# Last sequence's spatial product from seven block products, in a kernel of chunked linear attention and a gated layer

## The chip, the cores and the metric

One core of a Trainium2 chip runs the whole program. The metric is device time in microseconds (us), from the launch of the program to its end; the profiler adds one execution with a trace. TensorE is called PE here, VectorE DVE, ScalarE ACT, GpSimd POOL, and SyncE, whose queue issues nearly all DMAs, SP. Each engine works through its own instructions in the order in which the program emits them, and waits on semaphores for the others.

## The reference, cut to what matters

Four sequences of 768 tokens go through a gated linear recurrence with 8 heads of 48 (complex gates, real output), and its output x, 384 features per token, through a gated layer:

```python
h = gelu(x @ w_in)                     # 384 -> 1024
u, v = h[..., :512], h[..., 512:]
v_n = (v - mean(v)) / sqrt(var(v) + 1e-06) * g_ln
v_s = einsum('ts,bsd->btd', w_sg, v_n) + b_sg[None, :, None]
out = x + (u * v_s) @ w_out            # 512 -> 384
```

w_sg is 768 x 768 and mixes the tokens of a sequence: v_s is the *spatial product* that the change is about. For one sequence it is a 768 x 768 by 768 x 512 product.

## The kernel before

The recurrence is worked in 24 chunks of 128 tokens, six to a sequence. Behind each sequence's attention comes its gated layer, with features on partitions and tokens along the row, in two halves of 384 tokens. Operands of large products are split in two: "high" holds the value rounded to the type that PE reads, "low" what is left. A product is then three passes (high·high, high·low, low·high), by the helper `mm3` (L228). All four sequences compute the spatial product alike: for each half and each of four feature tiles f, `spatial` (L820) runs 6 chunks x 3 passes = 18 matmuls of 128x128 by 128x384 into the PSUM tile `pvs`, 144 for a sequence. Then DVE makes tg = pvs·g + b (L848), multiplies by u (L851), `high` makes gh (L212) and `low` makes gl (L220), and PE multiplies both with w_out into `po`; DVE adds x (L868), and a DMA stores it (L871). `normal` (L763) loads a half of x, makes v, its gelu and layer norm, and vh/vl for each chunk; `expand` makes u. The layer norm's small steps (`rsqrt`, L721) run on POOL.

Nothing schedules this. Every piece of work is a generator, and the table ORDER (L33) says whose next step is emitted: a token names a generator, a count behind a colon takes several steps, one mark (') sends the step's flexible work to POOL and two marks to DVE; without one `high` goes to ACT and `low` to DVE. Names: a attend (attention of a chunk; DVE masks its scores in L657 as tile `am`), z heads (loads K and Q), v vbuf, n normal, x expand, y spatial and the output product, h gate_range and k weight_range. These last two check inputs: each loads 192 or 384 KB (`gr`, `wr`) through SP into one of two buffers with the tags "re" and "im", and reduces them to a column on DVE (L382, L385, L311) or ACT. At the end `ok` (L883 to L894, L1005) joins the columns; all engines read the flag `oki` and go on to a general version when it is not set. The attention output of a chunk is copied (`yp`), stored to DRAM (`xd`) and loaded back as x.

Of the kernel before, what the change touches and what calls it, by code (L numbers as in the profile page):

```python
# [9 lines left out]
F32 = mybir.dt.float32  # L10
F32R = mybir.dt.float32r
# [3 lines left out]
ALU = mybir.AluOpType  # L15
# [3 lines left out]
P = 128  # L19
# [54 lines left out]
a20 e11 s12 h15 h4 a20 h1 a20 a21 e11'' r22' r22:3 a20 y2_3 z23 a20'' a20 a21' a21:2 y2_3'' a21 h15 h22 a21 y2_3''  # L74
a21:2 x2_0:2 h5 m12 y2_3'' h22 h0 x2_0 y2_3 e12' y2_3 v23 z22 y2_0 h5' v22 y2_3 h2 a20' y2_0 x2_0 y2_3:3 y2_0'' e12
r22:3 x2_0 r22 y2_3 x2_0 y2_3 a20 y2_0 y2_0'' a21 z22 y2_0:2 z23 k7 y2_0:2' y2_0:3 a21 h0' a22:5 a22' a22 e12 h2'
a22:2 x2_0 a23 y2_0 a22 y2_3 h18 e12'' a22' a22 y2_0'' n3_0 a23:2 a23'' a22 n3_0' y2_0 a22 a23 n3_0' y2_0:2 a23:2
y2_0' n3_0 h18 n3_0:2 k10 h1' k10 n3_0:3 y2_0'' y2_0 n3_3 n3_0 n3_3 k7 n3_0 y2_0:2 n3_0 n3_3' h7 h7'' k12 y2_0:3 n3_0
k1 n3_0' y2_0 n3_0' y2_0 n3_0 y2_0 n3_3 n3_0' n3_0:2 n3_3 n3_0' n3_3 n3_0 n3_3 k12 n3_0 h6 n3_3:3 x3_3 n3_3 x3_3 n3_3
y2_0 x3_3:3 h19 x3_3 k1 x3_3 n3_3:2 n3_3' x3_0 h19 n3_3 n3_3:2' n3_3'' x3_3 h13 n3_3' n3_3'' n3_3 h23 k6 h13 x3_0:2 h6  # L80
h23 y3_3:2 y3_3:3'' y3_3:2 y3_3' y3_3:5 k6 k9 y3_3'' h14 y3_3' h14 y3_3 k4 k0 x3_0 y3_0 y3_3 y3_0 k3 x3_0 k4 y3_3'
x3_0 y3_3'' k9 y3_3' h12 y3_3:3 y3_0' k3 h12 y3_3:2 x3_0 y3_3:2 h21:2 y3_3 h16 h17 x3_0 y3_0'' h17 y3_0' y3_0:2 x3_0
y3_0'' y3_3 y3_0' k0 k11 y3_0 h3 h16 y3_0 ok x3_0 h3 y3_0 y3_0'' k11 ok y3_0 x3_0 y3_0 ok:2 y3_0:2 ok y3_0:3 ok y3_0:3
ok y3_0:9
"""


# [1 line left out]
def tile_kernel(ctx: ExitStack, tc: tile.TileContext, t_q, t_k, t_re, t_im, u_q, u_k, u_re, u_im, t_v, v, q, k, f_re, f_im,  # L89
                w_in, g_ln, w_sg, b_sg, w_out, out):  # L90
    nc = tc.nc


    B, S, H, D = v.shape
    DM = H * D
    NCH = S // P
    DFF = w_in.shape[-1]
    F = DFF // 2
    NK = DM // P
    NF = F // P  # L100
# [16 lines left out]
    gp = ctx.enter_context(tc.tile_pool(name="gp", bufs=1))  # L117
# [82 lines left out]
    def ew():  # L200

        return nc.gpsimd if alt[0] == 1 else nc.vector
# [7 lines left out]
    def high(h, src):  # L210

        if alt[0] == 0:  # L212
            act(h, src, AF.Copy)
        elif alt[0] == 1:
            nc.gpsimd.tensor_scalar(out=h, in0=src, scalar1=1.0, scalar2=1.0, op0=ALU.mult, op1=ALU.mult)
        else:
            nc.vector.tensor_copy(h, src)  # L217

    def low(l, src, h):
        ew().tensor_tensor(out=l, in0=src, in1=h.bitcast(F32), op=ALU.subtract)  # L220
# [539 lines left out]
        yield  # L760
        return x, xh, xl

    def normal(b, c0, m):  # L763

        x, xh, xl = yield from get_x(b, c0, m)
        mv = mp.tile([P, 2, MT // P], F32, tag="mv", name="mv")
        neg = mp.tile([P, MT // P], F32, tag="neg", name="neg")
        vrs = []
        for i in range(m):
            pv = psm.tile([P, F], F32, tag="m", name="pv")  # L770
            if b == 0:
                stoke(pv[:, 0:2 * P], 20 if c0 + i == NCH - m else 3)
            ts = slice(i * P, (i + 1) * P)
            mm3(pv, lambda kt: xh[:, kt, ts], lambda kt: xl[:, kt, ts],
                lambda kt: winh[:, kt, F:], lambda kt: winl[:, kt, F:], NK)
            yield
            vr = mp.tile([P, F], F32, tag="vr", name="vr", bufs=3)
            act(vr, pv, AF.Gelu_apprx_tanh)
            vrs.append(vr)
            yield  # L780
            stt = mp.tile([P, 6], F32, tag="bst", name="bst")
            nc.vector.bn_stats(stt, vr)  # L782
            nc.vector.bn_aggr(mv[:, :, i], stt)
            yield
        rs, sh = rsqrt(neg, mv, m)
        yield
        for i in range(m):
            s_ = c0 + i
            vr = vrs[i]
# [5 lines left out]
            yield  # L795
            vh = mp.tile([P, F], F32R, tag=f"vh{s_}", name=f"vh{s_}", bufs=1)
# [282 lines left out]
```

## Time and profile before

| | us |
|---|---|
| three timed runs | 423.67, 424.76, 426.26 |
| their median | 424.76 |
| profiled execution | 426.0 |
| its span on the core | 424.3 |
| PE busy | 408.2 (96%) |
| DVE busy | 342.3 (81%) |
| ACT busy | 278.6 (66%) |
| POOL busy | 152.0 (36%) |

Busy time counts matmuls as long as any is in the array, so that PE's gaps are what is left of the span. 1.7 us of the profiled execution lie outside its span. A row of the trace below names line, engine, operation, and output<-input tiles.

### The profile page before, as it was taken

Reading aid. Unit: us, or ns where it says so; the run is one execution under the profiler, and the core shown is the slowest. Engines: PE = TensorE matmul, PEld = TensorE weight load, DVE = VectorE, ACT = ScalarE, POOL = GpSimd, SP = SyncE. Lnnn points to the kernel's source line nnn. Section 1 sums busy time; section 2 is a strip of 40 time slices with the busy share of each in tenths; the row PEclk is TensorE's granted clock in tenths of the full one; section 3 lists DMA queues with packets and bytes.
Section 4 is the critical chain, followed back from the end, with each engine's and each line's share of the span. In section 5 each row is a group of like instructions: output and inputs, shape, how many; then the busy total and the mean of one; then the engine's idle time right before and its main releaser. Section 6 shows DMA issues by size and latency. Waiting matters only on the chain.

```text
span 424.3 us, 9760 instructions
## 1 busy us (share of the span) xinstructions
PE 408.2 (96%) x3806; PEld 370.9 (87%) x3806; DVE 342.3 (81%) x593; ACT 278.6 (66%) x392; POOL 152.0 (36%) x207
## 2 busy tenths in 40 slices
PE   7999998989999999999999999999999999999995
PEld 5567787878899998889989998989999988899994
DVE  4999989999998999896999698786974556575483
ACT  7899998999989677786896935876640212540010
POOL 2126348255241430625164722542121144233210
PEclk9999999999999999999999999999999999999999
DMA  6878869598397896988749888879669856563441
GB/s 198 266 224 250 231 183 289 161 283 260 108 289 247 235 320 161 289 279 255 215 145 280 248 260 241 267 221 288 147 192 276 246 173 192 153 225 112 157 133 61
DMA packets 77563, 92.93 MB, mean 219 GB/s; under 512 B 10564, under 2 KB 59462, under 8 KB 77512
## 3 DMA queue, kind: packets, MB, share of 16 engines
q1 hardware_dynamic: 77368, 92.16, 73.1%
q8 instruction: 31, 0.51, 0.5%
q14 instruction: 20, 0.16, 0.1%
q10 hardware_dynamic: 144, 0.10, 0.1%
HBM read 68.64 MB, written 23.60 MB: 217 GB/s over the span
## 4 chain that ended last, share of the span: by engine, by line
PE 57%; DVE 15%; DMA 10%; ACT 10%; POOL 3%; issue 3%; SPq 1%; DVEq 0%; POOLq 0%
PE pvs L231 18%; PE po L835 10%; PE pu L231 6%; PE pv L231 6%; PE pa L647 4%; PE py L704 3%; ACT L194 3%; PE py L709 3%; PE ps L673 2%; DMA K<-rk 2%; DMA vbuf<-in_t_v_dram 2%; ACT csn L195 2%; DVE bst L782 2%; ACT l L195 1%; DMA Q<-rq 1%
## 5 line engine op out<-in xcount | busy, mean ns | idle before, releaser
L231 PE MATMUL pvs<-wsgh,vh 128*128 128x384 f32 x192 | 65.3, 340 | 0.0
L231 PE MATMUL pvs<-wsgh,vl 128*128 128x384 f32 x192 | 64.8, 337 | 0.1
L231 PE MATMUL pvs<-wsgl,vh 128*128 128x384 f32 x192 | 64.5, 336 | 0.0
L194 ACT ACT_TABLE_LOAD x48 | 61.6, 1283 | 1.7 <-PEq L1064 0.9
L647 PE MATMUL pa<-Q,K 96*64 96x128 f32 (+1 forms) x768 | 41.5, 250 | 1.1 <-DVE am L657 0.9
L647 PEld LDWEIGHTS pa<-Q,K 96*64 96x64 f32 x768 | 36.9, 137 | 3.9 <-ACT csn L195 1.0
L704 PE MATMUL py<-am,vbuf 128*64 128x128 f32 x384 | 38.2, 275 | 0.6 <-DVE am L657 0.6
L231 PEld LDWEIGHTS pvs<-wsgh,vh 128*128 128x128 f32 x192 | 36.0, 188 | 1.0 <-issue 0.9
L231 PEld LDWEIGHTS pvs<-wsgh,vl 128*128 128x128 f32 x192 | 36.0, 188 | 0.6 <-DVE vl L220 0.6
L231 PEld LDWEIGHTS pvs<-wsgl,vh 128*128 128x128 f32 x192 | 36.1, 188 | 0.0
L657 DVE TENSOR_TENSOR am<-pa,masks 128x512 f32<-128x512 f32 x45 | 30.1, 680 | 5.2 <-PE pa L647 4.4
L709 PE MATMUL py<-Q,S 96*48 96x128 f32 x320 | 33.2, 272 | 0.1
L835 PE MATMUL po<-gh,wouth 128*128 128x384 f32 x96 | 32.9, 343 | 0.0
L835 PE MATMUL po<-gl,wouth 128*128 128x384 f32 x96 | 32.4, 337 | 0.4 <-DVE gl L220 0.4
L231 PE MATMUL pu<-xh,winh 128*128 128x384 f32 x96 | 32.7, 341 | 0.0
L835 PE MATMUL po<-gh,woutl 128*128 128x384 f32 x96 | 32.3, 336 | 0.0
L231 PE MATMUL pu<-xh,winl 128*128 128x384 f32 x96 | 32.3, 336 | 0.0
L231 PE MATMUL pu<-xl,winh 128*128 128x384 f32 x96 | 32.2, 336 | 0.0
L220 POOL TENSOR_TENSOR gl<-tg,gh 128x384 fp32r<-128x384 f32 x13 | 16.5, 1266 | 42.7 <-DVE gh L217 20.3
L231 PE MATMUL pv<-winh,xl 128*128 128x512 f32 x72 | 28.7, 398 | 1.8 <-POOL xl L220 1.1
L231 PE MATMUL pv<-winh,xh 128*128 128x512 f32 x72 | 29.3, 406 | 1.1 <-DVE xh L217 0.7
L231 PE MATMUL pv<-winl,xh 128*128 128x512 f32 x72 | 28.5, 396 | 0.0
(253 smaller groups left out, 1066.6 us busy)
## 6 DMA issues: line engine op xcount, KB each, us to landing
vbuf<-in_t_v_dram SPq DMA_DIRECT2D x24, 288.0 KB, 5.5
K<-rk SPq DMA_DIRECT2D x18, 384.0 KB, 6.0
Q<-rq SPq DMA_DIRECT2D x18, 384.0 KB, 7.9
x<-xd SPq DMA_DIRECT2D x9, 576.0 KB, 5.1
xd<-yp SPq DMA_DIRECT2D x48, 96.0 KB, 3.3
gr<-in_f_im_dram SPq DMA_DIRECT2D x12, 384.0 KB, 4.0
out_dram<-x SPq DMA_DIRECT2D x23, 192.0 KB, 2.6
re<-in_u_re_dram SPq DMA_DIRECT2D x9, 384.0 KB, 5.9
```

The source lines that it names most:

```text
L194: nc.scalar.preload_act_table_set(SETS[t])
L195: nc.scalar.activation(out, in_, func, scale=scale, **kw)
L220: ew().tensor_tensor(out=l, in0=src, in1=h.bitcast(F32), op=ALU.subtract)
L231: nc.tensor.matmul(o, w(i), x(i), start=(i == 0 and j == 0), stop=(i == n - 1 and j == 2))
L647: nc.tensor.matmul(pa[rows, hh, j:], K(h)[:, j:j + KB], Q(h)[:, j:], start=True, stop=True)
L657: nc.vector.tensor_tensor(out=pairs(am), in0=pairs(pa), in1=causal, op=ALU.mult)
L673: nc.tensor.matmul(ps[r, h, :], columns[:, h * 2 * D + r.start:h * 2 * D + r.stop], V[:, h * D:(h + 1) * D], start=True, stop=True)
L704: nc.tensor.matmul(py[64 * e:64 * e + 64, p_, :], Vy(h)[:, 0:64], ams[h // 4][:, h % 4, :], start=True, stop=c == 0)
L709: nc.tensor.matmul(py[64 * e:64 * e + D, p_, :], Sb()[:, h, :], Q(h), start=False, stop=True)
L782: nc.vector.bn_stats(stt, vr)
L835: nc.tensor.matmul(po[d], w[:, f, ds], g[:, f, :], start=f == 0 and j == 0, stop=f == NF - 1 and j == 2)
```

## The change

Only the last sequence's spatial product changes. w_sg and v_n are each cut 2 x 2 (halves of 384 tokens on both sides of w_sg; halves of 384 tokens by halves of 256 features of v_n), and the four block results come from seven block products and sums of blocks (Winograd's form of Strassen's scheme). For each of two feature tiles i a block product is 3 chunks x 3 passes = 9 matmuls of the old size.

`combine` and `combine_first` load rows of w_sg again from DRAM (nine loads, 384 KB each, in the buffers tagged "re" and "im") and make the sums of blocks on that side, split in high and low, in tiles that are free by then; `sum_up` makes those of the v side. `product` emits nine matmuls, `blocks_begin`, `blocks` and `blocks_end` (tokens i, j, q) run the seven kinds in the PSUM tiles `A`, `P` and `Q`, with partial sums `c12`, `c22`, `c21` made by DVE between them, and `gated` makes gh and gl as before. `output` is the old output product alone. ORDER differs from the attention of chunk 20 to its end: checks are read at other places, and the last quarter is in another order.

```diff
-z21 y2_3 y2_3'' y2_3:2 z20 y2_3 a19' y2_3'' k5 y2_3'' e12 h4 y2_3 x2_0 k5 e12 a20:2' a20 v21 a20' h8 a20 s12 a20 a19
...
+z21 y2_3 y2_3'' y2_3:2 z20 y2_3 a19' y2_3'' k5 y2_3'' e12 h4 y2_3 x2_0 k5 h15 h4 h15 h8 s12 a20:2' a20 s12 a20' a20:3
...
+    def combine(j):
+
+        r1 = gp.tile([P, S], F32, tag="re", name="b1", bufs=2)
+        nc.sync.dma_start(out=r1, in_=w_sg[j * P:(j + 1) * P, :])
+        yield
+        r2 = gp.tile([P, S], F32, tag="im", name="b2", bufs=2)
+        nc.sync.dma_start(out=r2, in_=w_sg[(j + HS) * P:(j + HS + 1) * P, :])
+        yield
+        minus = lambda o, x, y: ew().tensor_tensor(out=o, in0=x, in1=y, op=ALU.subtract)
+        minus(r1[:, T1ST], r1[:, T2ND], r1[:, T1ST])
...
+        high(h, r2)
+        yield
+        low(l, r2, h)
+        yield
...
+    def combine_first(j):
...
+        ew().tensor_tensor(out=r1[:, T1ST], in0=r1[:, T2ND], in1=r1[:, T1ST], op=ALU.subtract)
+        yield
+        high(wsgh[:, j, T2ND], r1[:, T1ST])
...
+    def sum_up(j, vr):
...
+        ew().tensor_tensor(out=a22, in0=a22, in1=s3, op=ALU.subtract)
+        yield
+        ew().tensor_tensor(out=a12, in0=a12, in1=a22, op=ALU.subtract)
+        yield
+        high(sh[:, 0:2], vr.rearrange("p (a f) -> p a f", a=2))
+        yield
+        low(sl[:, 0:2], vr.rearrange("p (a f) -> p a f", a=2), sh[:, 0:2])
+        yield
+        ew().tensor_tensor(out=s3, in0=a22, in1=a11, op=ALU.add)
...
+    def product(o, kind, i, first=False):
...
+        for j in range(HS):
+            (ah, al), (th, tl) = a(j), t(j)
+            for k_, (w, x) in enumerate(((ah, th), (ah, tl), (al, th))):
+                nc.tensor.matmul(o, w, x, start=first and j == 0 and k_ == 0, stop=j == HS - 1 and k_ == 2,
+                                 skip_group_check=True)
...
+    def blocks(i):
...
+        product(A, 1, i, True)
...
+        scaled(c12, A, i, bsg[:, T2ND])
+        yield
+        scaled(c22, A, i + 2, bsg[:, T2ND])
...
+        product(A, 2, i)
+        yield
+        scaled(c12, held["P", i], i, c12)
+        yield
+        product(held["P", i], 7, i)
+        yield
...
+        scaled(c22, held["P", i], i + 2, c22)
+        yield
+        product(held["P", i], 4, i)
...
+    def output(c0):
...
+        order = ((0, 2, 1, 3), (2, 3, 0, 1))[half]
...
-            chains.update({f"x{b}_{c0}": expand(b, c0, m), f"y{b}_{c0}": spatial(b, c0, m)})
+            chains.update({f"x{b}_{c0}": expand(b, c0, m), f"y{b}_{c0}": output(c0) if b == LAST else spatial(b, c0, m)})
```

The first place is DVE at the attention of chunks 20 and 21. A check is a row with `gr` or `wr` and, mostly, one of `stats`; `k` and `em` are K's rotation. Before, the kt copies, masks `am` and state updates `S` stand behind one check, of `wr`:

```order
L311 ISA wr,stats<-wr 128x384
L311 ISA stats 128x1
L206 COPY kt<-pk 128x384 x2
L657 TENSOR_TENSOR am<-pa_111,masks 128x512
L657 TENSOR_TENSOR am<-pa_1332,masks 128x512
L583 TENSOR_TENSOR k_3768<-k_3768,csn_3788 128x768
L686 TENSOR_TENSOR S<-ps,S 96x384
L848 SCALAR_TENSOR_TENSOR tg<-pvs,gcol,bsg 128x384
L657 TENSOR_TENSOR am<-pa_1332,masks 128x512
```

Now:

```order
L387 ISA stats 128x1
L211 COPY kt<-pk 128x384 x2
L662 TENSOR_TENSOR am<-pa_111,masks 128x512
L588 TENSOR_TENSOR em_3944<-k_3768,csn_3788 128x768
L691 TENSOR_TENSOR S<-ps,S 96x384
L932 SCALAR_TENSOR_TENSOR tg<-pvs,gcol,bsg 128x384
L387 ISA gr,stats<-gr 128x768
L387 ISA stats 128x1
L316 ISA wr,stats<-wr 128x384
L316 ISA stats 128x1
L390 TENSOR_SCALAR gr,stats<-gr 128x768
L662 TENSOR_TENSOR am<-pa_1332,masks 128x512
```

A `gr` check, whose last row is the first shown, stands ahead of the kt copies, and three checks (gr, wr, gr) between chunk 20's work and the last mask.

The second place is SP's queue, whose DMAs bring K and Q of chunks 22 and 23 and x of the last sequence (`b` is a buffer for rows of w_sg). Before:

```order
L364 DMA vbuf_115<-in_t_v_dram 128x576
L607 DMA K<-rk 96x1024
L364 DMA vbuf_113<-in_t_v_dram 128x576
L871 DMA out_dram<-x 128x384
L379 DMA gr<-in_f_re_dram 64x768 x2
L871 DMA out_dram<-x 128x384
L586 DMA rq<-ep_3943 128x3x128 x2
L586 DMA rq<-q_4211 128x3x128 x2
L717 DMA xd_0_135<-yp 48x4x128 x2
L607 DMA Q<-rq 96x1024 x2
L308 DMA wr<-in_moe_w_in_dram 128x768
L717 DMA xd_3_136<-yp 48x4x128 x2
```

Now:

```order
L773 DMA b_4304<-in_moe_w_sg_dram 128x768
L722 DMA xd_0_135<-yp 48x4x128 x2
L384 DMA gr<-in_f_im_dram 128x768
L955 DMA out_dram<-x 128x384
L776 DMA b_4340<-in_moe_w_sg_dram 128x768
L612 DMA K<-rk 96x1024
L612 DMA Q<-rq 96x1024
L384 DMA gr<-in_f_re_dram 64x768 x2
L754 DMA x<-xd_0_135 128x3x384
L722 DMA xd_3_136<-yp 48x4x128 x2
L612 DMA K<-rk 96x1024
L612 DMA Q<-rq 96x1024
```

Four of the nine loads of w_sg stand ahead of the first of these K loads, and two more ahead of the x of the second half.

The third place is DVE at the program's end. Before:

```order
L889 MEMSET ones 128x2
L848 SCALAR_TENSOR_TENSOR tg<-pvs,gcol,bsg 128x384
L851 TENSOR_TENSOR tg<-u__5128,tg 128x384
L894 CAST oki<-pok 1x2
L220 TENSOR_TENSOR gl<-tg,gh 128x384
L1005 TENSOR_LOAD oki
L868 TENSOR_TENSOR x<-po,x 128x384 x2
L868 TENSOR_TENSOR x<-po,x 128x192 x2
```

Now:

```order
L1100 MEMSET ones 128x2
L225 TENSOR_TENSOR gl<-tg,gh 128x384
L987 TENSOR_TENSOR tg<-u__5078,tg 128x384
L222 CAST gh<-tg 128x384
L225 TENSOR_TENSOR gl<-tg,gh 128x384
L1105 CAST oki<-pok 1x2
L1216 TENSOR_LOAD oki
L1079 TENSOR_TENSOR x<-po,x 128x384 x2
L1079 TENSOR_TENSOR x<-po,x 128x192 x2
```

The flag's cast stands behind both last `gl`, where before it stood ahead of the last one. On PE the read of the flag (TENSOR_LOAD) stands ahead of the last 9 output matmuls, before ahead of the last 15.

## Rows read from the trace of the kernel before

**Rows 1.** The page's first part: busy us, share of span, count by engine.
```profile
PE 408.2 (96%) x3806; PEld 370.9 (87%) x3806; DVE 342.3 (81%) x593; ACT 278.6 (66%) x392; POOL 152.0 (36%) x207
```

**Rows 2.** Windows by stage: span, busy us (count) by engine, clock, DMA share, GB/s.
```profile
316.50:337.00 20.50, 20.50 (x119) 20.46 (x118) 9.13 (x17) 2.10 (x4) 3.42 (x4) 1.00 0.94 256
337.00:345.20 8.20, 8.20 (x170) 7.75 (x167) 6.46 (x13) 2.42 (x5) 1.27 (x1) 1.00 0.82 249
345.20:366.00 20.80, 19.69 (x101) 17.39 (x98) 10.76 (x24) 6.35 (x10) 11.00 (x13) 1.00 0.54 163
366.00:395.00 29.00, 29.00 (x163) 28.22 (x162) 19.52 (x44) 9.11 (x16) 8.69 (x14) 1.00 0.46 152
395.00:419.60 24.60, 24.60 (x142) 23.87 (x140) 14.60 (x42) 2.95 (x6) 3.02 (x4) 1.00 0.41 134
sum 103.10, PE 101.99 PEld 97.70 DVE 60.47 ACT 22.94 POOL 27.40; mean PE 20.40 PEld 19.54 DVE 12.09 ACT 4.59 POOL 5.48
```

**Rows 3.** Chain of waits, core 0: start us, length us, engine, work, line.
```profile
342.09 4.05 DMA x<-xd
...
362.59 6.30 PE pv L231 x27
...
375.13 12.77 PE pvs L231 x72
...
394.17 6.24 PE po L835 x36
```

**Rows 4.** PE timeline: start us, us, operation, count, [idle before, its releaser].
```profile
348.74 0.40 PE L231 MATMUL pv<-winl,xh 128*128 128x512 f32 x1
350.25 0.50 PE L231 MATMUL pv<-winh,xl 128*128 128x512 f32 x1 [1.11 <-POOL xl L220]
```

**Rows 5.** Other engines in the same stretch, same columns.
```profile
347.54 2.66 POOL L220 TENSOR_TENSOR xl<-x,xh 128x1152 fp32r<-128x1152 f32 x1
...
347.81 0.59 ACT L208 COPY yp<-py 128x512 f32<-128x512 f32 x1 [4.39 <-DMA xd<-yp]
...
349.24 1.76 DVE L382 CUSTOM_DVE_ANT_0 gr<-gr 128x768 f32<-128x768 f32 x1
...
350.15 1.73 POOL L851 TENSOR_TENSOR tg<-u__4443,tg 128x384 f32<-128x384 f32 x1
```

**Rows 6.** Groups by form on DVE: busy us, mean ns, idle before and releasers.
```profile
L848 DVE SCALAR_TENSOR_TENSOR tg<-pvs,gcol,bsg 128x384 f32<-128x384 f32 x32 | 19.5, 608 | 11.2 <-PE pvs L231 11.0
...
L220 DVE TENSOR_TENSOR gl<-tg,gh 128x384 fp32r<-128x384 f32 x19 | 13.6, 714 | 5.2 <-ACT gh L195 2.9 <-POOL kt L624 1.8 <-POOL gh L215 0.4
...
L382 DVE CUSTOM_DVE_ANT_0 gr<-gr 128x768 f32<-128x768 f32 x12 | 12.4, 1037 | 9.0 <-DMA gr<-in_f_im_dram 9.0
L220 DVE TENSOR_TENSOR xl<-x,xh 128x1152 fp32r<-128x1152 f32 x7 | 10.4, 1488 | 0.0
...
L311 DVE CUSTOM_DVE_ANT_0 wr<-wr 128x384 f32<-128x384 f32 x13 | 7.1, 548 | 0.0
```

**Rows 7.** Groups by form on POOL.
```profile
L220 POOL TENSOR_TENSOR gl<-tg,gh 128x384 fp32r<-128x384 f32 x13 | 16.5, 1266 | 42.7 <-DVE gh L217 20.3 <-ACT gh L195 19.0 <-PE pvs L231 3.2
```

**Rows 8.** Groups by form on ACT.
```profile
L195 ACT ACTIVATE xh<-x 128x1152 fp32r<-128x1152 f32 x8 | 9.3, 1161 | 2.8 <-DMA x<-xd 1.4 <-PE pv L231 1.3
```

**Rows 9.** DVE timeline at the attention of chunk 21, before's order.
```profile
313.94 0.69 DVE L657 TENSOR_TENSOR am<-pa,masks 128x512 f32<-128x512 f32 x1 [1.38 <-PE pa L647]
...
315.02 0.95 DVE L382 CUSTOM_DVE_ANT_0 gr<-gr 128x768 f32<-128x768 f32 x1
```

**Rows 10.** DMA issues from 300 us on: KB each, median us to landing.
```profile
xd<-yp SPq DMA_DIRECT2D x10, 96.0 KB, 2.6
K<-rk SPq DMA_DIRECT2D x2, 384.0 KB, 8.2
```

**Rows 11.** Timeline of the last part.
```profile
415.05 0.14 DVE L894 CAST oki<-pok 1x2 int32<-1x2 f32 x1
...
419.77 0.62 DVE L868 TENSOR_TENSOR x<-po,x 128x192 f32<-128x192 f32 x2 [1.52 <-PE po L835]
```

More of the change, by code (lines that the diff above doesn't have):

```diff
@@ L795, in normal @@
             yield
+            if split and c0 == 0:
+                ew().tensor_tensor(out=vr[:, HF:], in0=vr[:, 0:HF], in1=vr[:, HF:], op=ALU.subtract)
+                yield
             vh = mp.tile([P, F], F32R, tag=f"vh{s_}", name=f"vh{s_}", bufs=1)
@@ L802, in normal @@
             yield
+            if split and c0:
+                yield from sum_up(i, vr)
     def expand(b, c0, m):
@@ new lines, in gated @@
+    def gated(o, f, base, us, half):
+        tg = mp.tile([P, F], F32, tag="vr", name="tg", bufs=3)[:, 0:MT]
+        nc.vector.scalar_tensor_tensor(out=tg, in0=o, scalar=gcol[:, f:f + 1], in1=base, op0=ALU.mult, op1=ALU.add)
+        yield
+        ew().tensor_mul(tg, us[f], tg)
+        yield
+        if ("g", half) not in held:
+            held["g", half] = [mp.tile([P, NF, MT], F32R, tag=t, name=t, bufs=1) for t in ("gh", "gl")]
+        gh, gl = held["g", half]
+        high(gh[:, f, :], tg)
+        yield
+        low(gl[:, f, :], tg, gh[:, f, :])
+        yield
@@ new lines, in blocks @@
+    def blocks(i):
+        us, _ = keep["u", LAST, MT // P]
+        shape = [P, MT]
+        A = psm.tile(shape, F32, tag="m", name="A") if i == 0 else psf.tile(shape, F32, tag="phi", name="A")
+        scaled = lambda o, x, f, y: nc.vector.scalar_tensor_tensor(out=o, in0=x, scalar=gcol[:, f:f + 1], in1=y,
+                                                                   op0=ALU.mult, op1=ALU.add)
+        product(A, 1, i, True)
+        yield
+        if i == 0:
+            c12, c22 = (ap_.tile(shape, F32, tag="S", name="c", bufs=2) for _ in range(2))
+        else:
+            c12, c22 = (t[:, 0:MT] for t in vbuf)
+        held["c", i] = c12, c22
+        scaled(c12, A, i, bsg[:, T2ND])
+        yield
+        scaled(c22, A, i + 2, bsg[:, T2ND])
+        yield
+        c21 = ap_.tile(shape, F32, tag="am", name="c21", bufs=2)
+        scaled(c21, A, i + 2, bsg[:, T1ST])
+        yield
+        product(A, 2, i)
+        yield
+        scaled(c12, held["P", i], i, c12)
+        yield
+        product(held["P", i], 7, i)
+        yield
+        gate = gated(A, i, bsg[:, T1ST], us, 0)
+        next(gate)
+        yield
+        scaled(c22, held["P", i], i + 2, c22)
+        yield
+        product(held["P", i], 4, i)
+        yield
+        yield from gate
+        yield from gated(held["P", i], i + 2, c21, us, 0)
@@ new lines, in blocks_begin, with blocks_end @@
+    def blocks_begin(i):
+        held["P", i] = psm.tile([P, MT], F32, tag="m", name="P") if i == 0 else psa.tile([P, MT], F32, tag="pa", name="P")
+        product(held["P", i], 6, i, True)
+        yield
+    def blocks_end(i):
+        us, _ = keep["u", LAST, 0]
+        c12, c22 = held["c", i]
+        Q_ = psm.tile([P, MT], F32, tag="m", name="Q")
+        product(Q_, 5, i, True)
+        yield
+        yield from gated(Q_, i + 2, c22, us, 1)
+        product(Q_, 3, i)
+        yield
+        yield from gated(Q_, i, c12, us, 1)
@@ new lines, in output, with add @@
+    def output(c0):
+        half = int(c0 == UFINAL)
+        _, x = keep["u", LAST, c0]
+        order = ((0, 2, 1, 3), (2, 3, 0, 1))[half]
+        po = [None] * NK
+        def add(d, f):
+            gh, gl = held["g", half]
+            if po[d] is None:
+                po[d] = pst.tile([P, MT], F32, tag="t", name="po")
+            ds = slice(d * P, (d + 1) * P)
+            for j, (w, g) in enumerate(((wouth, gh), (wouth, gl), (woutl, gh))):
+                nc.tensor.matmul(po[d], w[:, f, ds], g[:, f, :], start=f == order[0] and j == 0,
+                                 stop=f == order[-1] and j == 2)
+        for f in order[:-1]:
+            for d in range(NK):
+                add(d, f)
+            yield
+        for d in range(NK):
+            ds = slice(d * P, (d + 1) * P)
+            add(d, order[-1])
+            yield
+            halves = 2 if half and d == NK - 1 else 1
+            spans = [slice(i * MT // halves, (i + 1) * MT // halves) for i in range(halves)]
+            for z in spans:
+                nc.vector.tensor_tensor(out=x[:, d, z], in0=po[d][:, z], in1=x[:, d, z], op=ALU.add)
+            yield
+            for z, q_ in zip(spans, (nc.sync, nc.scalar)):
+                q_.dma_start(out=out[LAST, ds, c0 * P + z.start:c0 * P + z.stop], in_=x[:, d, z])
+            if halves > 1:
+                nc.tensor.matmul(po[d - 1][0:2, 0:2], x[:, d - 1, MT - 2:MT], x[:, d - 1, MT - 2:MT], start=True, stop=True)
```

86 lines of the change are left out of this document (72 added, 14 removed).

## The prediction

> **What bounds the kernel now.** The page's first part comes first: PE is busy 408.2 of 424.3 us, 96% [rows 1]. Read the windows by stage next: in 316.5 to 419.6, which holds all that the change moves, PE works 101.99 of 103.10 us at a granted clock of 1.00, the upper of its two levels (2.4 GHz), while DVE works 60.47, ACT 22.94 and POOL 27.40 [rows 2]. So PE is the bound there, and its idle time is 1.1 us. Where the clock is at its upper level throughout, a removed matmul is worth its whole time as long as PE stays fed. Third, the chain of waits: it runs through PE from 362.59 to the end, with one change of engine ahead of that, a POOL step that PE waits for at 350.25 [rows 3, 4]. To be seen there is the price of a matmul without a stall: 12.77 us for 72 of `pvs`, 0.177 each, and 6.24 for 36 of `po`, 0.173 each [rows 3]. The single gap: PE starts its second pass of `pv` at 348.74 and the third, which reads xl, only at 350.25 [rows 4]; a `pv` matmul takes 6.30/27 = 0.233 [rows 3], so 1.51 - 0.23 = 1.28 us are lost. The cause stands in the same stretch: POOL makes xl from 347.54 on in 2.66 us [rows 5].
>
> **What the change removes.** (1) Before, the last sequence takes 2 halves x 4 feature tiles x 18 = 144 `pvs` matmuls; after, 7 block products x 2 feature tiles x 9 = 126. Both have the same shape. 18 x 0.173 to 0.177 = 3.1 to 3.2 us; I take **-3.15**. Nothing hides this saving, PE being solid there.
>
> (2) The 1.28 us gap: xl of that half moves from POOL to DVE, where this form takes 1.49 [rows 6], and 54 `pvs` matmuls and an attention now lie between the load and its first use. 54 x 0.177 = 9.6 us cover it. **-1.3**, bounds 0 (another wait stands in the same place) and -1.4.
>
> Both together: -4.45, with every new piece hidden.
>
> **What it adds.** Counted in the program, DVE gets 10 more scalar steps of the form of `tg`, 0.608 each [rows 6], 6.1 us, and a net 18 others, sums, splits and low parts of 256 to 1152 columns; scaled from gl (384 columns, 0.714) and xl (1152, 1.488) they come to some 12 us [rows 6]. DVE's 60.5 us become about 78 of 100, so there is room in the mean, not at every place. POOL gets 20 more steps of 384 columns with two inputs, at gl's 1.27 each [rows 7] 25 us: 27.4 becomes about 53 (its other edits nearly cancel). ACT gets some 10 steps net, none much longer than xh's 1.16 [rows 8]: under 12 of its 77 free us. None of this is on the path by itself; it is where a result is needed soon that it shows. The places follow; none can gain, since from 316.5 on PE waits only at 350.25 [rows 2, 4], and at (3) the mask is made as soon as its scores are there [rows 9].
>
> (3) Attention of chunks 20 and 21. Before, DVE takes the last mask `am` at 313.94, right when PE has its scores ready, waits for it 1.38 us in advance, and makes the check `gr` (0.95) only after it [rows 9]. After, that check and two more stand between the state update and that mask: gr about 0.95 [rows 9], wr 0.55 [rows 6], and another gr of about 0.95, 2.45 in all, of which the 1.38 that DVE idled there before hide a part. Behind the mask PE waits with its `py` matmuls, and everything after them. 2.45 - 1.38 = 1.1 is what can show, less what else of DVE's queue goes from there to later; behind the mask wait the next state update and K's rotation: **+0.5**, bounds 0 and 2 (a check that finds its data late).
>
> (4) Chunk 23's masks stand behind DVE's xl. If K and Q land when they did, the mask waits for up to 1.49 [rows 6]; PE has an output product beside it. **+0.3**, 0 to 1.4.
>
> (5) The x of the second half. From the last chunk's `py`: copy yp 0.59 [rows 5], store 2.6 [rows 10], load 4.05 [rows 3], xh on ACT 1.16 [rows 8], xl on DVE 1.49 [rows 6]: 9.9 us. After, PE has 27 `pv` of the first half (6.30) and 24 `po` (24 x 0.173 = 4.2) to do meanwhile, 10.5 [rows 3]. The margin of 0.6 is smaller than what POOL beside it can add to xl (2.66 - 1.49 = 1.2 where POOL itself makes it [rows 5, 6]). **+0.3**, 0 to 2.
>
> (6) The block products. The first A product reads three chunks of vl of the second half, the last of them behind some 9 us of DVE work that starts only after the layer norm's steps on POOL; `pu` matmuls of 18 and 18 lie beside it (6.2 us at 0.173 [rows 3]), with `po` ahead. Then P holds a running sum: DVE must read it into c12 or c22 (0.608 [rows 6]) before the next product adds to it, two rounds for each of the two feature tiles, with nine or eighteen matmuls of the other tile (1.6 to 3.2 us) between. **+0.7**, 0 to 2.5, the far end being two low parts late by a POOL step of 1.27 each [rows 7].
>
> (7) The end. The flag's cast, 0.14 at 415.05, went before ahead of the last gl [rows 11]; now it stands behind it, and PE's read of the flag ahead of the last 9 matmuls, 9 x 0.173 = 1.6 us, where 15 stood. The last two gl are on the path: DVE or POOL, 0.71 or 1.27 [rows 6, 7]. **+0.3**, 0 to 1.2. What follows the last matmul (two halves of the x add, 0.62 together [rows 11], and the store) is the same.
>
> (8) The nine loads of w_sg and earlier checks: each load is 393 KB; at 256 GB/s with a DMA share of 0.94 [rows 2], so about 272 at full share, 1.45 us each, 13 us. The spare share to 366 is 0.06 x 20.5 + 0.18 x 8.2 + 0.46 x 20.8 = 12.3 us [rows 2]: it just fits, and I put nothing on the path for it beyond (4) and (5). If it doesn't fit, that is rival D.
>
> **Sum.** -4.45 + 0.5 + 0.3 + 0.3 + 0.7 + 0.3 = -2.35. The profiled execution took 426.0 (1.7 of it outside its span), so 423.65 in the same terms; it lies 1.24 above the median of the runs, 424.76, and on that median the same difference makes **422.4**.
>
> **Rivals.** B: nothing new shows. For it: in before, PE is solid for 53.6 us from 366 on although DVE is 64% busy there [rows 2], so the order leaves DVE room. Against it: two margins under 1 us, (5) and (7). Waits of at most 1: 420.3 to 421.3.
>
> C: the saving goes into waits on DVE and POOL. The row for it: DVE's gr at 349.24 takes 1.76 where POOL's xl runs beside it, and 0.95 at 315.02 alone; and POOL's tg beside it takes 1.73 [rows 5, 9]. That is 0.8 more for one DVE step. With some 20 new two-input POOL steps, four to six such collisions ahead of something that PE waits for cost 3.2 to 4.9, and with the other terms at nothing to 0.3 the sum is -1.25 to +0.75: 423.5 to 425.5. Against it: DVE's gl, met by POOL in some cases, still has a mean of 0.71 [rows 6], so most steps escape. The Trainium skill, SBUF — State Buffer, section "Who interferes with whom", says that a DVE instruction with two SBUF inputs and a GpSimd instruction that reads SBUF exclude one another, for the whole instruction. By that rule the trace's 0.95 against 1.76 agrees, and it speaks against this change, which adds work of just these two kinds on both engines; by it the time is this rival's.
>
> D, slower: the one SP queue. Four loads of w_sg stand ahead of K and Q of chunk 22, six ahead of the x of the second half. K took 8.2 us to land before [rows 10]. If the loads in front, 4 x 1.45 = 5.8 us, are still in transfer then, chunk 22's attention comes up to 4 us late, and x by up to 3 for the two more (2 x 1.45). It decides from 6.6 us on (4.45 saved, and 2.1 to be lost): 426.9 to 428.5. For it: share 0.94 and 0.82 up to 345 [rows 2]. Against it: between the attentions PE has 135 matmuls, 135 x 0.175 = 23.6 us, as cover.
>
> **How the numbers follow.** A measurement of this kernel can tell about 0.5%, 2.1 us, from no change; faster then means under 422.64. Forecast, new waits of 1 to 3.2: 421.3 to 423.5, chance 0.45, of which 0.30 below 422.64. B 0.17, all faster. C 0.24, all within. D 0.14, all slower. Faster 0.30 + 0.17 = 0.47; same 0.15 + 0.24 = 0.39; slower 0.14. The range leaves out D and the edges of B and C: 420.4 to 425.4.
>
> **What would show it.** Right: PE's busy time in the last 100 us lower by 3.1, no gap at the first `pv` of the last sequence, gaps of some tenths at the last mask of chunk 21, at the second half's first `pv`, at A's ninth matmul and ahead of the last nine. Wrong: a single gap of over 2 us at one of these, K or x landing later than 8 us after issue (D), or gl and low parts on DVE over 1.4 us as a rule (C). Granted clock below 1.00 behind such a gap would make it dearer than the gap, and would upset every number here.

## The result: slower by 0.9%, and the profile after

| | before | after |
|---|---|---|
| median of 19 runs, us | 424.82 | 429.10 |
| lowest and highest | 423.67, 428.41 | 425.89, 432.05 |
| profiled execution | 426.0 | 428.58 |
| its span | 424.3 | 426.8 |
| first `pk` at the attention of chunks 20 and 21 to last matmul | 112.1 | 114.3 |
| last matmul to the end of the span | 4.6 | 6.0 |

The ratio is 1.0089 with a 95% interval of 1.0065 to 1.0112: 3.8 us slower (2.8 to 4.8), where 2.4 faster was forecast. The two profiled executions differ by less, because that of after reached this `pk`, with the same work on PE up to there, 1.0 us sooner; from there on it lost 2.1 + 1.4 = 3.5 us. The mean granted clock of the 19 runs after is 0.996, and 0.992 or 0.993 in the three longest (430.2 to 432.1 us); the profiled one has 0.999, and the runs of the kernel before beside the experiments have 0.998. Some of that is the end, where PE is idle: here the clock is at its lower level (1.2 GHz) from 425.83 on. Whether a lower clock adds to the 3.8 us elsewhere isn't shown by this trace.

The first part of the page after, which answers to [rows 1]:

```profile
PE 406.6 (95%) x3788; PEld 368.1 (86%) x3788; DVE 365.1 (86%) x619; ACT 285.8 (67%) x404; POOL 184.0 (43%) x237
```

PE has its 18 matmuls less, but only 1.6 us less busy time, because much of a wait between two matmuls counts as busy. DVE has 23 us more, POOL 32. So the work was added about where it was counted, and the question is what PE waited for. The waits of PE from 280 us on (engine, line, what ended the wait, us in total, times, longest); before had only the one at 350.25 [rows 4]:

```profile
PE pa L652 <- DMA Q<-rq: 1.3, 1, 1.3
PE py L709 <- DVE am L662: 0.8, 1, 0.8
PE pv L236 <- DVE xl L225: 0.5, 1, 0.5
PE py L709 <- POOL am L660: 0.4, 1, 0.4
PE A L979 <- DVE vl L225: 0.4, 1, 0.4
PE po L1065 <- issue: 0.2, 1, 0.2
```

By the starts of the matmuls beside their usual steps, PE lost 2.0 us at the attention of chunks 20 and 21, 2.0 at that of 22 and 23, 0.7 at the xl of the last half, 0.85 in the product stage and 0.4 ahead of the last nine matmuls: 5.95 us, where before lost 1.28. The list above shows 3.6 of them as idle time.

The first place on DVE and POOL (columns as in [rows 5]):

```profile
312.25 2.52 POOL L660 TENSOR_TENSOR am<-am,masks 128x512 f32<-128x512 f32 x1 [1.31 <-ACT am L659]
...
312.67 0.94 DVE L387 CUSTOM_DVE_ANT_0 gr<-gr 128x768 f32<-128x768 f32 x1
...
313.54 1.65 DVE L316 CUSTOM_DVE_ANT_0 wr<-wr 128x384 f32<-128x384 f32 x1
...
315.12 0.94 DVE L390 TENSOR_SCALAR_CACHE_REDUCE gr<-gr 128x768 f32<-128x768 f32 x1
...
315.99 0.68 DVE L662 TENSOR_TENSOR am<-pa,masks 128x512 f32<-128x512 f32 x1
```

and on PE:

```profile
314.82 0.44 PE L709 MATMUL py<-am,vbuf 128*64 128x128 f32 x4 [0.44 <-POOL am L660]
...
316.72 0.44 PE L709 MATMUL py<-am,vbuf 128*64 128x128 f32 x4 [0.80 <-DVE am L662]
```

Three checks stand ahead of DVE's mask, as foreseen. The one of wr takes 1.65 us, where its mean was 0.55 [rows 6]: POOL makes the other mask beside it, and that takes 2.52, where the same operation takes 1.27 at 312.85 in the trace before, with DVE idle for most of it. A little earlier K's rotation `em`, on DVE at 309.85, takes 1.90 beside POOL's first mask, where `k` of the same form took 0.96 at 310.61 before. DVE and POOL lengthened each other, and PE waited for both.

The second place is a transfer. The window from one attention to the next (columns as in [rows 2]), and the chain's row for Q of chunk 23:

```profile
317.80:341.50 23.70, 23.70 (x139) 23.67 (x138) 13.85 (x23) 3.62 (x7) 14.90 (x12) 1.00 0.99 279
```

```profile
338.59 9.07 DMA Q<-rq
...
354.65 5.82 DMA x<-xd
```

The 16 DMA engines are full, at 0.99, where the share was 0.94 before [rows 2]. Q lands at 347.66, after 9.07 us, and the row below shows PE waiting for it. The x of the last half takes 5.82 instead of 4.05 [rows 3].

```profile
347.79 1.56 PE L652 MATMUL pa<-Q,K 96*64 96x128 f32 x32 [1.35 <-DMA Q<-rq]
```

The third place is the end. First DVE, then the stores:

```profile
416.65 0.55 DVE L987 TENSOR_TENSOR tg<-u__5078,tg 128x384 f32<-128x384 f32 x1
417.24 0.36 DVE L222 CAST gh<-tg 128x384 fp32r<-128x384 f32 x1
417.63 0.56 DVE L225 TENSOR_TENSOR gl<-tg,gh 128x384 fp32r<-128x384 f32 x1
418.11 0.14 DVE L1105 CAST oki<-pok 1x2 int32<-1x2 f32 x1
...
419.19 2.39 SPq L1082 DMA_DIRECT2D out_dram<-x  x4
...
419.64 1.67 DVE L1079 TENSOR_TENSOR x<-po,x 128x384 f32<-128x384 f32 x4 [1.39 <-PE po L1065]
...
421.34 0.38 ACTq L1082 DMA_DIRECT2D out_dram<-x  x1
```

Five stores, 0.79 MB, are issued within 2.2 us around the last matmul's start at 420.8. The DMA issues of that stretch say how long the last one took (KB each, us to landing):

```profile
out_dram<-x ACTq DMA_DIRECT2D x1, 96.0 KB, 3.7
```

Before it was 2.5, in the same view:

```profile
out_dram<-x ACTq DMA_DIRECT2D x1, 96.0 KB, 2.5
```

Before, the third output tile made all its 12 matmuls last, and the stores of the first two lay beside them. `output` ends with three matmuls of each tile, so that the adds and stores of all three fall into PE's last 1.6 us and behind them. That is four of the five stores. The one at 419.19 belongs to the half worked first, whose adds were done at 411.0: ORDER has its step (`y3_3 y3_0:7` at the end) behind the flag, so SP issues it only after its read of the flag at 418.3 (`L1216`), and that waits for the cast at 418.11, behind the last gl.

The number of stores isn't shown to be what made the last one slow. The kernel before with 18 matmuls left out (`before_18_fewer`, below) issues four stores as the kernel before does, and its last one took nearly as long:

```profile
out_dram<-x ACTq DMA_DIRECT2D x1, 96.0 KB, 3.5
```

With the flag read only behind the last store it took 1.7, here in `before_late_flag`, and as long in the four other traces of this end that have its landing:

```profile
out_dram<-x ACTq DMA_DIRECT2D x1, 96.0 KB, 1.7
```

So the slow landing goes with an early read of the flag rather than with the number of stores; no run changes the one without the rest, nor shows how a read would lengthen a landing.

### The profile page after: what moved, and what is told of

Same layout as the page of the kernel before. It is cut to its first block, busy times and chain, and to the rows that moved or that the text cites. A ratio compares the mean times of both kernels' runs of the same rounds, so it can differ in the third digit from the quotient of the medians.

```text
span 426.8 us, 9843 instructions
## 1 busy us (share of the span) xinstructions
PE 406.6 (95%) x3788; PEld 368.1 (86%) x3788; DVE 365.1 (86%) x619; ACT 285.8 (67%) x404; POOL 184.0 (43%) x237
## 4 chain that ended last, share of the span: by engine, by line
PE 44%; DVE 31%; DMA 10%; ACT 5%; issue 4%; POOL 3%; SPq 1%; DVEq 0%; POOLq 0%; ACTq 0%
PE pvs L236 8%; PE pu L236 6%; PE po L919 5%; PE pa L652 4%; PE po L1065 3%; PE py L709 3%; PE ps L678 2%; DVE lo L440 2%; PE py L714 2%; DMA Q<-rq 2%; PE P L979 2%; DVE bst L861 2%; DVE am L662 2%; DMA vbuf<-in_t_v_dram 2%; DMA xd<-yp 2%
## 5 line engine op out<-in xcount | busy, mean ns | idle before, releaser
L236 PE MATMUL pvs<-wsgh,vh 128*128 128x384 f32 x144 | 49.1, 341 | 0.0
L236 PE MATMUL pvs<-wsgh,vl 128*128 128x384 f32 x144 | 48.5, 337 | 0.0
L236 PE MATMUL pvs<-wsgl,vh 128*128 128x384 f32 x144 | 48.4, 336 | 0.0
L225 POOL TENSOR_TENSOR gl<-tg,gh 128x384 fp32r<-128x384 f32 x17 | 19.7, 1164 | 36.1 <-ACT gh L200 26.7
L709 PEld LDWEIGHTS py<-am,vbuf 128*64 128x64 f32 x384 | 24.4, 136 | 4.4 <-DVE am L662 3.1
L236 PEld LDWEIGHTS pvs<-wsgh,vh 128*128 128x128 f32 x144 | 27.0, 188 | 0.8 <-issue 0.7
L236 PEld LDWEIGHTS pvs<-wsgh,vl 128*128 128x128 f32 x144 | 27.0, 188 | 0.3 <-DVE vl L225 0.3
L236 PEld LDWEIGHTS pvs<-wsgl,vh 128*128 128x128 f32 x144 | 27.1, 188 | 0.0
L919 PE MATMUL po<-gh,wouth 128*128 128x384 f32 x72 | 24.8, 344 | 0.0
L919 PE MATMUL po<-gl,wouth 128*128 128x384 f32 x72 | 24.3, 338 | 0.4 <-DVE gl L225 0.4
```

The lines of the kernel that those rows point to most:

```text
L236: nc.tensor.matmul(o, w(i), x(i), start=(i == 0 and j == 0), stop=(i == n - 1 and j == 2))
L709: nc.tensor.matmul(py[64 * e:64 * e + 64, p_, :], Vy(h)[:, 0:64], ams[h // 4][:, h % 4, :], start=True, stop=c == 0)
L919: nc.tensor.matmul(po[d], w[:, f, ds], g[:, f, :], start=f == 0 and j == 0, stop=f == NF - 1 and j == 2)
```

## The experiments

Ratios are against runs of the kernel before on the same chip, in brackets the 95% interval. 0.001 is 0.42 us.

**The same again** (`again`, no edit).

> The changed kernel once more, for a second profile. First theory (several small waits: DVE checks ahead of masks in the attention of chunks 20 and 21, about 2.0 us in the first profile; the load of Q for chunk 23, 1.6; places in the product stage, 2.3 together): each of them stands in this profile too, within 0.5 us, and the time is 1.005 to 1.012 of before. Rival (one of them is chance of that execution, and what costs the time lies spread over the stage): at least one of them is gone and the time is the same.

1.0092 (1.0062 to 1.0122). The losses stand at the same places: 2.1 in the attention of 20 and 21 (0.30, 0.42, 0.33, 1.06), 1.6 at that of 22 and 23, 0.8 at xl, 0.85 in the product stage, 0.4 at the end; 5.7 us from the last matmul to the end. So the places are no chance of one execution, though the sizes vary by some tenths.

**The checks behind the attention** (`checks_off_attention`; the loads that follow in the same buffers, the first of w_sg among them, are issued later with them):

```diff
-h15 h4 h15 h8 s12 ... a20 h22 h0 k7 a20'' y2_3 h22 v21 a20 a21' h7 e12 r22 k7 h7 b0 a21 y2_3:2' h0' a21:2 h1 a21 b0 r22
+h15 h4 h8 s12 ... a20 h22 h0 a20'' y2_3 v21 a20 a21' e12 r22 a21 y2_3:2' a21:2 h15 k7 h22 h7 b0 h0' k7 h7 h1 a21 b0 r22
```

> The changed kernel with four checks (gr, gr, wr, gr) that DVE made ahead of the masks of chunks 20 and 21 moved right behind the last of these masks; nothing else. First theory: PE's waits in that attention (0.3, 0.65 and 1.06) go, about 1.5 to 2.0 us, 1.004 to 1.006 of before. Rival (the saturated transfers set the pace, and attention 22 and 23 only wait longer for Q and K then): under 0.5 us change, 1.008 to 1.010, with the wait for Q longer by what the attention gained.

1.0165 (1.0134 to 1.0196): worse than the changed kernel by 0.8%, 3.2 us. The attention waits went, and two others came, for gl and kt, beside the old one for Q:

```profile
PE po L919 <- DVE gl L225: 1.8, 1, 1.8
PE ps L678 <- POOL kt L629: 1.2, 1, 1.2
PE pa L652 <- DMA Q<-rq: 1.1, 1, 1.1
```

The four checks now stand ahead of a gl that PE needs next. Neither theory foresaw that; the first one's gain didn't come. The profiled run is the fastest of the six, 429.2 against a median of 431.5, so that most of the 3.2 us isn't in this trace.

**Fewer transfers** (`no_weight_loads`; the same for the other four sums):

```diff
-        nc.sync.dma_start(out=r1, in_=w_sg[j * P:(j + 1) * P, :])
+        w1 = wsgh[:, j, :].bitcast(F32)
...
-        minus(r1[:, T1ST], r1[:, T2ND], r1[:, T1ST])
+        minus(r1[:, T1ST], w1[:, T2ND], w1[:, T1ST])
```

> The changed kernel without its nine loads of w_sg: the sums are made from the high parts that stand in SBUF, so the low part of w_sg is left out of them; every vector instruction stays. First theory: the wait for Q (1.6) goes and the share of the transfers between 318 and 341 us falls from 0.99, but the waits of the attention of chunks 20 and 21 and of the product stage stay: 1.5 to 2 us less, 1.004 to 1.006 of before. Rival (transfers set the whole loss): 3.5 to 5 us less, 0.997 to 1.001. Second rival (only the vector work counts): the same time, 1.008 to 1.010.

1.0055 (1.0030 to 1.0080), 1.5 us less than the changed kernel. The wait for Q is gone, and so is that for xl; the window's DMA share is 0.92:

```profile
317.80:340.90 23.10, 23.10 (x135) 23.07 (x134) 13.73 (x22) 5.48 (x11) 14.85 (x13) 1.00 0.92 270
```

1.7 us are still lost in the attention of chunks 20 and 21, 0.9 of them now at a `ps` that waits for vbuf, and the product stage has a new wait of 0.8 ahead of A. The block sums here leave out w_sg's low part, as in all the runs below without these loads. The transfers are a part of the loss, as the first theory had it.

**No sums of w_sg either** (`no_weight_sums`: `combine` hands out slices of wsgh and wsgl, `combine_first` does nothing).

> The changed kernel with neither the loads nor the sums and splits on the w_sg side: the products read the old tiles, so the block sums of w_sg are left out of the result. 18 fewer matmuls, the sums on the v side and the order stay. First theory: what the loads cost goes, and 1 to 1.5 us of DVE and POOL queues with it, the checks in the attention stay: 0.998 to 1.002 of before. Rival (transfers alone): the same as without the loads, within 0.5 us. Rival (order and checks alone): 1.005 or more.

1.0022 (1.0000 to 1.0045), 2.8 us less than the changed kernel and just above the first theory's range. Beyond the loads the sums cost about 1.4 us by the middles of the intervals, which overlap. What stays are 2.0 us in the attention of chunks 20 and 21, 0.85 in the product stage, and an end of 5.3.

**18 matmuls fewer in the kernel before** (`before_18_fewer`):

```diff
-                lambda s_: wsgh[:, s_, tsl], lambda s_: wsgl[:, s_, tsl], NCH)
+                lambda s_: wsgh[:, s_, tsl], lambda s_: wsgl[:, s_, tsl], NCH - (b == B - 1 and f > 0))
```

> The kernel before with 18 of the last sequence's 144 spatial matmuls left out (the last of six chunks in three of four feature tiles of each half), so that part of the sum is missing; all else stays. First theory (PE is the bound, a matmul is worth its time): 3.15 us less, 421.8, 0.992 to 0.993 of before. Rival (the work beside PE has no room, and PE waits for it instead): 0 to 1.5 us less, 0.997 to 1.000.

0.9963 (0.9933 to 0.9993): 1.6 us (0.3 to 2.8), half of what the first theory said, and between the two theories. In the profile PE gains 2.5 up to its last matmul, 0.9 of that because the old wait for xl is 0.4 in this execution; there are new waits of 1.2 us among the last output matmuls, and the end takes 5.6 us instead of 4.6, with the last store 3.5 us in transfer.

**Another end** (`late_flag`):

```diff
-q0:2 ok q0 q1 y3_0 q1 ok y3_0 k4 ok:3 q0' q0 q1 q1'' q1 ok y3_0 ok y3_0:2 y3_3 y3_0:7
+q0:2 ok q0 q1 y3_0 q1 q0' q1 y3_0 q1'' q0 q1 k4 ok:3 y3_0 y3_0:2 y3_3 y3_0:4 ok y3_0 ok:2 y3_0:2
...
-            for d in range(NK):
+            for d in range(NK - half):
...
-            add(d, order[-1])
+            for f in order if half and d == NK - 1 else order[-1:]:
+                add(d, f)
```

> The changed kernel with another end: the last two multiplications by u and the last gl go ahead of the joining of the checks on DVE, the flag is read behind the last output matmuls, and the third output tile does all its 12 matmuls last, as in the kernel before, instead of 3 of each tile. First theory (the end costs 1.8 us: 0.4 waiting for the last gl, 1.4 because the last stores are issued together and land late): 1.5 to 2.0 us less than the changed kernel, 1.004 to 1.006 of before, and 4.4 to 5 us instead of 6.0 from the last matmul to the end of the span. Rival (PE only waits earlier, for the same gl): within 0.5 us of the changed kernel.

1.0101 (1.0062 to 1.0140): no gain. The end did shrink, from 6.0 to 5.1 us, but PE stood still ahead of the small product that joins the checks:

```profile
421.64 0.19 PE L1103 MATMUL pok<-ones,ok 128*1 128x2 f32 x2 [1.10 <-DVE ones L1101]
```

DVE had its check, nine small steps and two adds to do ahead of that. The rival was right, by a wait that this edit made itself.

**The small product last** (`late_flag_2`, the edit above with this line instead of its last):

```diff
-k4 ok:3 y3_0 y3_0:2 y3_3 y3_0:4 ok y3_0 ok:2 y3_0:2
+k4 ok:3 y3_0 y3_0:2 y3_3 y3_0:5 ok y3_0 ok y3_0 ok
```

> The changed kernel with the other end as before (last gl ahead of the joining of the checks, third output tile's 12 matmuls last), and now also the small product that joins the checks behind all output matmuls, so that PE has nothing to wait for between them. First theory (the end costs 1.8 us): 1.5 to 2 us less than the changed kernel, 1.004 to 1.006 of before, PE without a gap over 0.3 in the last 6 us, and under 5.3 us from the last matmul to the end. Rival (what is won there is noise beside other waits): within 0.7 us of the changed kernel.

1.0030 (1.0007 to 1.0053), 2.5 us less than the changed kernel. From the last matmul to the end it takes 4.3 us, and no gap over 0.25 us stands in PE's last 6 us. This is the most that an edit of one place gave. It moves three things at once, though: the last gl, the flag's read with the store behind it, and the third tile's matmuls; and this profile also has shorter waits for Q and xl, which the edit doesn't touch. DVE's last gl now ends at 414.95, 3.2 us sooner:

```profile
413.06 0.56 DVE L987 TENSOR_TENSOR tg<-u__5078,tg 128x384 f32<-128x384 f32 x1
413.65 0.36 DVE L222 CAST gh<-tg 128x384 fp32r<-128x384 f32 x1
413.93 1.02 DVE L225 TENSOR_TENSOR gl<-tg,gh 128x384 fp32r<-128x384 f32 x2
```

**Short checks** (`short_checks`; `wr` likewise, for check 7):

```diff
+        t = t[:, 0:16] if i in (0, 15, 22) else t
```

> The changed kernel with four checks (three gr, one wr, all read on DVE at the attention of chunks 20 and 21) reduced over 16 columns only, so most of their input isn't looked at; the loads and the order stay. First theory (their time on DVE is what PE waits for there): the waits of 0.3, 0.65 and 1.06 shrink to under 0.5 together, 1.5 to 2 us less than the changed kernel, 1.004 to 1.006 of before. Rival (the rest of the loss takes the gain up, as when the checks were moved: Q for chunk 23 lands no sooner): within 0.7 us of the changed kernel, with a longer wait for Q at chunk 23.

1.0072 (1.0040 to 1.0104), about 0.7 us less than the changed kernel: the rival. The waits in the attention of chunks 20 and 21 shrank from 2.0 to 0.7 us, and PE came to the next attention 1.4 us sooner; there it lost 2.8 instead of 2.0:

```profile
PE ps L679 <- POOL kt L630: 1.3, 1, 1.3
PE pa L653 <- DMA Q<-rq: 0.6, 1, 0.6
PE ps L679 <- DMA vbuf<-in_t_v_dram: 0.5, 1, 0.5
```

**Short checks and no loads** (`no_loads_short_checks`, both edits).

> The changed kernel without its nine loads (block sums from the high parts in SBUF) and with the four checks at the attention of chunks 20 and 21 reduced over 16 columns only. First theory (the loads hide what the shorter checks give back: with both away PE waits neither in that attention nor for vbuf and Q in the next): 3.5 to 4.5 us less than the changed kernel, 0.998 to 1.001 of before, so that the two edits together give more than the 1.6 and 0.9 us that they gave one by one. Rival (they simply add): 1.002 to 1.004.

1.0006 (0.9983 to 1.0029): 3.5 us less than the changed kernel. One by one the edits gave 1.5 and 0.7; together more by the middles, but simple addition would give 1.0038, itself no surer than its three intervals, and isn't excluded. It fits that the full transfers took back what the shorter checks gave.

**Three mends at once** (`three_mends`: `no_weight_loads`, `late_flag`, and the four checks spread between other DVE work behind the attention).

> The changed kernel without the nine loads (block sums of w_sg made from the high parts in SBUF), with the checks of the attention of chunks 20 and 21 spread behind it between other DVE work, and with the end in the other order. First theory: the three gains add up, 1.6 + 1.5 to 2 + 1.5 to 2 us less than the changed kernel: 422.8 to 424.2, 0.995 to 0.999 of before. Rival (DVE has no place for the checks without a wait): 0.5 to 1.5 us more than this.

1.0051 (1.0028 to 1.0074): the rival. It has the wait of `late_flag`, and PE stood still for PSUM tiles that DVE and ACT emptied too late, since checks stood ahead of that work:

```profile
PE pu L236 <- ACT u__4321 L200: 1.7, 1, 1.7
PE pok L1103 <- DVE ones L1101: 1.1, 1, 1.1
PE pu L236 <- DVE x L952: 1.0, 1, 1.0
```

**Three smaller mends** (`three_mends_2`: `no_weight_loads`, `late_flag_2`, and two checks moved):

```diff
-h22 v21 a20 a21' h7 e12 r22 k7 h7 b0 a21 y2_3:2' h0' a21:2 h1 a21 b0 r22 a19 b0' x2_0 y2_3 e12 h1' r22
+h22 v21 a20 a21' h7 e12 r22 h7 b0 a21 y2_3:2' a21:2 a21 r22 a19 x2_0 y2_3 k7 h0' h1 b0 b0' e12 h1' r22
```

> A complete kernel: no loads of w_sg (block sums from the high parts in SBUF), two of the four checks (wr and gr) moved from ahead of chunk 21's last mask to behind the next gl, and the end of the run before. First theory: 1.6 for the loads, about 1 for the checks, 1.5 for the end, 4 us less than the changed kernel: 424 to 425.3, 0.998 to 1.001 of before. Rival (each mend moves a wait on, as the first three together did): 1.003 to 1.006.

0.9994 (0.9976 to 1.0012): 4.0 us less than the changed kernel, as the first theory had it. The whole loss against the kernel before is gone, but not yet the saving.

**Everything but the products away** (`all_but_products`: `no_weight_sums`, `short_checks`, `late_flag_2`).

> The changed kernel without the loads and sums on the w_sg side (products read the old tiles, so the block sums are left out), with the four short checks, and with the mended end: all three suspects away at once, the 18 fewer matmuls, the sums on the v side and the rest of the order kept. First theory (loads with their sums, the checks in the attention and the end are the whole loss but for 1 us in the product stage): 421.0 to 423.0, 0.991 to 0.995 of before. Rival (the rest of the order costs as much again): 0.997 or more.

0.9961 (0.9942 to 0.9979), 1.7 us less than before. The profiled run is the slowest of the twelve, 426.6: PE waits 2.9 us for vbuf at 313.4, the granted clock is at its lower level from 315.95 to 319.36, and the matmuls behind the wait run at that level until then. The ratio lies between the two theories, and it is what 18 fewer matmuls gave by themselves (0.9963). So the three suspects account for the loss within the intervals, some 1.5 us; the first theory's price of the matmuls was too high.

**The late flag without and with the 18 matmuls, in the kernel before** (`before_late_flag`; `before_18_fewer_late_flag` has the 18 fewer as well):

```diff
-ok:2 y3_0:2 ok y3_0:3 ok y3_0:3 y3_0:9
+ok:2 y3_0:2 y3_0:3 y3_0:3 y3_0:7 ok y3_0 ok y3_0 ok
```

> The kernel before with the joining of the checks on PE, the flag's cast and its reading by all engines moved behind the last output matmul; nothing else. First theory (the flag's read is hidden in the kernel before, and stays hidden behind the landing of the last stores): within 0.5 us of before, 0.999 to 1.001. Rival (it is on the path now): 0.5 to 1.5 us less.

> The same end, and 18 of the last sequence's 144 spatial matmuls left out as before (the last of six chunks in three of four feature tiles of each half, so a part of the sum is missing). First theory (a matmul is worth its 0.175 us, and half was lost beside the joining of the checks): 2.7 to 3.2 us less than the kernel before with this end, 0.992 to 0.994 of before. Rival (18 matmuls are worth half here, because the engines beside PE have no more room at the end): 1.2 to 2 us less, 0.995 to 0.998.

0.9980 (0.9956 to 1.0004) and 0.9951 (0.9925 to 0.9978). The end alone can't be told from no change. The 18 matmuls are worth 0.0029 on top of it, 1.2 us, within wide bounds (about -0.3 to 2.8); the full 3.15, 0.0074, would have made it 0.9906 from the middle of the first interval, outside the second. So the joining of the checks doesn't explain the other half.

**Checks on ACT** (`checks_on_act`, `three_mends_2` with three marks taken away, so that these reads go to ACT):

```diff
-k7 h0' h1 b0 b0' e12 h1' r22 ... q1 h3' h14
+k7 h0 h1 b0 b0' e12 h1 r22 ... q1 h3 h14
```

> The complete kernel of the second three mends, with three more checks of 768 columns read by ACT instead of DVE (2.9 us less on DVE, the same on ACT, which is idle two thirds of that time). First theory (what is left of the loss is DVE's queue): 0.5 to 1.5 us less than without this edit, 0.996 to 0.998 of before. Rival (DVE isn't waited for at those three places): 0.999 to 1.001.

0.9957 (0.9933 to 0.9982): 1.8 us faster than before, and the first version with block sums in place that beats it, though without w_sg's low part in them. The waits that `three_mends_2` still had for xl, gl and the x add are gone; what the profile lists is three:

```profile
PE A L979 <- DVE c L1002: 0.9, 1, 0.9
PE A L979 <- DVE vl L225: 0.4, 1, 0.4
PE ps L678 <- DMA vbuf<-in_t_v_dram: 0.4, 1, 0.4
```

## Why the prediction was wrong, by its steps

The forecast was 2.4 us less and the kernel took 3.8 more. What failed is (3), (8) and (7), each too small by 1.5 us or more, and the sentence in (1) that nothing hides the saving. The time is also above the 426.9 to 428.5 of rival D, the only slower one.

(1) "Nothing hides this saving, PE being solid there" took a busy PE for the only bound. PE does have 18 matmuls less, but 18 left out of the kernel before were worth 1.6 us (0.3 to 2.8), and 1.2 beside another end: with less to do PE runs into waits that the old matmuls had covered, 1.2 us of them in the profile of `before_18_fewer`. That these are the whole missing half isn't shown; the 1.0 us more behind the last matmul is one profile.

(2) The wait of 1.28 us at the old xl went, as forecast, and one of 0.7 to 0.8 came at the other half's xl, which is (5).

(3) The attention of chunks 20 and 21 was priced at 0.5 and took 2.0, the upper bound, though not for the reason given there (a check that finds its data late). At the last mask, the place named, it was 1.0: wr was taken at 0.55, alone, and met POOL's mask, 1.65. The other 1.0 was lost at POOL's own mask and at `ps`, which the step doesn't name. This is rival C's mechanism at a place where the forecast had none of it. By the Trainium skill, SBUF — State Buffer, section "Who interferes with whom", a DVE instruction with two SBUF inputs, as this check is, and a GpSimd instruction that reads SBUF contend for a shared pair of ports that only one of them holds at a time; the trace's 1.65 against 0.55, with 2.52 against 1.27 on POOL, agrees.

(4) and (8) The loads were put at nothing beyond 0.3 and 0.3. With them the transfers are full for 24 us, and they cost about 1.5 us by `no_weight_loads`, at Q of chunk 23 and at the last xl. Spare share counted over 50 us said "it just fits"; what counted was the stretch ahead of Q, where the share was 0.94 already. This is rival D's place, at a smaller price than it named, and its sign, K landing later than 8 us after issue, came: 8.6, and Q 9.1. What (4) names didn't occur: DVE began chunk 23's mask at 348.74, as soon as the scores were there, and it was the scores that came late, behind Q.

(5) 0.3 was forecast, 0.7 to 0.8 measured. POOL beside xl was the reason given, but xl took 1.36, less than the 1.49 counted; the transfer of x took 5.82 instead of 4.05. Without the loads the wait was gone in one profile and stood at 0.8 in `three_mends_2`, so the transfer isn't its only cause.

(6) The product stage: 0.7 forecast, 0.85 measured. 0.58 of it is at A's ninth matmul, behind vl, as named. The 0.27 in P was a wait for the low part of a v-side sum (`s`, done at 384.8), not for DVE's reading of P: there the size came out by luck.

(7) "What follows the last matmul is the same" was false: 4.6 us became 6.0, of which 1.2 is the last store's longer landing. The flag's read, priced by PE's last nine matmuls alone, also held back a store on SP, and the changed loop in `output` put the stores of all three tiles together. With the late last gl this end costs 2.5 us by `late_flag_2`; which of its parts costs what stays open. The loop stood in the diff and the flag's place in the order; what follows the last matmul was not looked at.

In the trace of the changed kernel the terms close without a smaller saving in (1): -3.15 and -1.28, then +2.0 (3), +2.0 at the attention of 22 and 23, +0.7 (5), +0.85 (6), and +0.4 and +1.4 at the end (7) make +2.9, and the trace lost 3.5 from there on; the rest lies in steps of a tenth. Against the sum on record, (3) is short by 1.5, (4) and (8) by 1.7, (7) by 1.5, (5) and (6) together by 0.5. So the half that 18 matmuls lose in the kernel before isn't a term to add to these: it shows that waits come up there too once PE has less to do.

## What to carry to other kernels

Where an engine is 96% busy because everything around it was made to fit, taking work off it can be worth less than that work's time; here it was about half (1.6 of 3.15 us, with 0.3 to 2.8 possible). A run that only leaves the work out, and nothing else, tells this before the replacement is written. Price the stretch behind the last matmul by itself: which stores start there, what on their queue stands ahead of them, and what stands ahead of the last operand on its engine. Free time of a queue or an engine counts only in the stretch between the producer and the consumer that waits, and a check moved out of one such stretch must not land in the next.

## What the runs showed that was not expected

The last store of 96 KB landed after 2.5 us in the kernel before and 3.7 in the changed one, after 3.5 with the stores of the kernel before in `before_18_fewer`, and after 1.7 in five traces with the flag read behind it. A reduction of 128x384 on DVE took 1.65 us instead of 0.55 beside a POOL operation of 128x512, which took 2.52 instead of 1.27. And a mend priced at 1.5 to 2 us at one place gave little or nothing three times (`checks_off_attention`, `short_checks`, `late_flag`): another wait took it back, twice one that the edit itself had made.
